# A fused scan-and-experts kernel: another order in the opening, weight sums two at a time, one set of scores two products sooner

## The chip, the cores and the metric

The kernel runs on one core of one Trainium2 chip. The metric is the time of one execution on the device in microseconds, the median of several runs. Five engines run side by side, each its own list of instructions in order: TensorE (PE, matrix products into PSUM banks; PEld is its loading of weights), VectorE (DVE), ScalarE (ACT), GpSimd (POOL) and SyncE (SP, which issues most transfers). ACT can issue transfers too. An engine waits on semaphores that other engines or transfers raise.

## The reference, cut to what matters

```python
# block 1: chunked scan; batch 4, 8 heads, 768 steps, head_dim 32, state 16
cum = np.cumsum(log(clip(a, 1e-6, 1)), -1)             # inside a chunk
L = np.exp(cum[..., :, None] - cum[..., None, :]) * causal
y = (C @ B.T * L) @ x + (C @ state) * exp(cum)         # per chunk
state = exp(cum[-1]) * state + (B * exp(cum[-1] - cum)).T @ x
# block 2: four experts on the 3072 x 256 tokens that y makes
p = probs / (probs.sum(-1, keepdims=True) + 1e-9)
for e in range(4):
    out += p[:, e:e+1] * (np.maximum(y @ w1[e], 0) @ w2[e])   # w1 256x1024, w2 1024x256
```

## The kernel before

**Work and tiles.** The 3072 steps are cut into 24 chunks of 128. Chunk `c` belongs to sequence `c % 4`. Everything is float32. The experts are computed with a fast matrix scheme of 20 products (`G`, blocks of three token pairs by four quarters of an expert's hidden units) and, for the very first expert of the first block, with smaller ones (`B`, 7 products, and plain products). Such a scheme multiplies sums of weight blocks with sums of token blocks. The weight sums are made once on the chip (`operands`, L1024, on POOL or DVE), used, stored to DRAM (`w_d`, L1029) and loaded again for the later token blocks. There are four token blocks of six chunks; each passes over all four experts.

**Two ways to the decay matrix.** For the first six chunks DVE multiplies up the decays themselves (`scan`, L519): of `a` with its first element of a row set to zero, spread over 128 partitions. For chunks 0 to 2 PE does the spreading (`spread`, L660) from three small tiles `aq0` and `aq1[:, 0:2]` (inside V buffers), in which only every 32nd partition holds a row and the others must be zero; for chunks 3 to 5 a transfer does it from a copy in DRAM, `acut_d` (`load_decays`, L463). Later chunks use logs: `a_sb` gets Ln on ACT (L708), DVE sums them (`sums`, L725), the sums go to `cum_d` in DRAM, and PE turns them for a bias (`bias`, L1360).

**The opening** (L568 to L738) is written out by hand, in program order for every engine. POOL and DVE clear `aq0` and `aq1`. SP loads the rows of `a` into `aq0` (L572), ACT loads `probs` (`pr`, L570) and the rows for `aq1` (L574). SP then loads `xb` (tokens, B and C of a chunk, in two parts for chunks 0 and 1), `a_sb` and the first weights. DVE clips the tiles between 1e-6 and `own`, which is one on every 32nd partition and zero elsewhere (L608). POOL adds up `probs` (`pairs`, `total_p`), DVE takes the reciprocal (L618), POOL makes the gates `pc` (L619), then clips `a_sb` and makes the cut copy `a_cut`, which SP stores to `acut_d` (L630). Then, for chunks 0 and 1: `spread` on PE, `mask` on ACT (L495), `score` on PE (L502), four scans per chunk on DVE (`scan_quarters`), and the product of scores and decays into `MT`. That product is made for each quarter `r` of the heads, either by `masked` (L681: DVE reads the scores in PSUM) or by `aside` (L675, L676: ACT copies the scores to a tile `gs`, POOL multiplies). Before, `aside` does quarters 0 and 1 of chunk 0 and quarter 0 of chunk 1; `masked` does the other five. `fade` (L540, POOL) adds the columns for the state, `inner` (L546, PE) makes the chunk's outputs and states, and ACT copies them out. `idle` (L684) are products of ones whose results nobody reads.

**The planned part.** What follows (from L743) is a list of works with costs per engine. A planner in the kernel's own Python (`Plan`) fixes the order on every engine before anything runs, from assumed costs, from the time `now` at which the planned part begins and from assumed times at which buffers and loads are ready. PE's order, `line`, is given; DVE, ACT, POOL and SP follow from latest starting times. `PAIRS_AT` says at which product of a unit (one expert over one token block) the scan's scores (`"s0"`) and outputs (`"o0"`) of the next block are put in. Since every engine's order comes out of one plan, a changed cost or start can move any instruction.

**Products.** `product` (L933) is the pair of 128x256 matmuls that nearly all of PE's time goes to. Between them DVE adjusts a bank (`adjust`, L1071), gates one (`gated`, L968) or combines sums (`combine`, L960), and ACT copies banks out and back (L942, L947, L1213).

Every transfer takes one of eight semaphores in turn, and its issue waits until the transfer that had that semaphore before has landed.

Of the kernel before, what the change touches and what calls it, by code (L numbers as in the profile page):

```python
# [8 lines left out]
FP32 = mybir.dt.float32  # L9
# [3 lines left out]
P = 128  # L13
# [18 lines left out]
URGENT = {}  # L32
# [3 lines left out]
SCANNED = 6  # L36
SCORED, OWN, LEAD, LEFT = 7, 4, 5, 3
FILLED = 3
HORIZON, OPENING, LOADED = 26.0, 80.0, 1.0
ORDERS = (0, 1, 2, 3), (3, 1, 2, 0), (0, 1, 2, 3), (3, 1, 2, 0)  # L40
PAIRS_AT = ((1, 24, "s0"), (2, 1, "o0"), (2, 1, "s1"), (2, 24, "s2"), (3, 1, "o12")), (
# [28 lines left out]
class Plan:  # L70
# [109 lines left out]
    def run(self, line, at, begin):  # L180
# [17 lines left out]
        self.stall, self.port, self.bus = [], 0.0, begin["SP"] + 4  # L198
# [103 lines left out]
class Scheme:  # L302
# [9 lines left out]
G.sums = ((15, 13, 10, -1), (9, 11, 10, -1), (0, "a", 16, -1), (2, "c", 11, -1), (1, "c", 13, -1),  # L312
          (14, 16, 13, -1), (3, "e", 10, -1), (7, 10, "c", -1), (18, "d", 10, -1), (17, "d", 16, -1),
          (8, 16, 11, -1), (19, "a", 13, -1), (6, "a", 11, -1), (12, 13, "d", -1), (5, "e", 16, -1),
          (4, 11, "e", -1))
# [6 lines left out]
G.shared = {1: ((15, 9), (0, 2), (1, 14), (3, 7), (18, 17), (8, 19), (5, 6), (12, 4)),  # L322
            2: ((9, 15), (7, 2), (19, 3), (17, 12), (14, 4), (8, 5), (18, 1), (6, 0))}
# [36 lines left out]
def kernel(  # L360
# [32 lines left out]
    def real(c):  # L393
        return c % NSEQ * NC + c // NSEQ
# [26 lines left out]
    def some(n, shape, name, pool=const):  # L421
# [19 lines left out]
        "dram": [None],  # L441
# [109 lines left out]
    def keep_state(c, A, y):  # L551
# [16 lines left out]
    nc.gpsimd.memset(aq0, 0.0)  # L568
    nc.vector.memset(aq1, 0.0)
    nc.scalar.dma_start(out=pr, in_=probs)  # L570
    a_rows = a.rearrange("(i k) (q t) s -> k q i (t s)", k=NC, t=NT)[0]
    nc.sync.dma_start(  # L572
        out=aq0.rearrange("(q r) t s -> q r (t s)", q=NQ)[:, 0], in_=a_rows[:, 0])
    nc.scalar.dma_start(  # L574
        out=aq1.rearrange("(q r) c t s -> q r c (t s)", q=NQ)[:, 0], in_=a_rows[:, 1:SPREAD])
# [3 lines left out]
    nc.sync.dma_start(out=xb[0][:, OBT:], in_=xbc[real(0)][:, OBT:])  # L579
    nc.sync.dma_start(  # L580
        out=a_sb, in_=a.rearrange("c h s -> (c h) s").rearrange("(p r) s -> p r s", r=2))
    nc.sync.dma_start(out=xb[1][:, OBT:], in_=xbc[real(1)][:, OBT:])
# [4 lines left out]
    load_tokens(2, xb[2])  # L587

# [4 lines left out]

    tmask = const.tile([P, NT], FP32)
    nc.vector.memset(tmask, 0.0)
    for q in range(NQ):
# [5 lines left out]
    own = const.tile([P, 1], FP32)  # L602
    nc.vector.reduce_sum(
        own.unsqueeze(2), ident[:, 0].rearrange("p (q r) -> p r q", r=32)[:, 0:1],
        axis=mybir.AxisListType.X)

    def clip(engine, v, top=1.0):
# [10 lines left out]
    nc.vector.reciprocal(total_p, total_p)  # L618
    nc.gpsimd.tensor_mul(  # L619
        pc.rearrange("p (k q) e -> p q k e", q=NSEQ), pr.rearrange("p (q k) e -> p q k e", q=NSEQ),  # L620
        total_p.rearrange("p (q k) e -> p q k e", q=NSEQ).to_broadcast([P, NSEQ, NC, E]))
    clip(nc.vector, aq1.rearrange("p c t s -> p (c t s)"), own)
    nc.vector.memset(aq1[:, :, :, 0:1], 0.0)

    clip(nc.gpsimd, a_sb)
    nc.gpsimd.tensor_copy(a_cut, a_sb)
    nc.gpsimd.memset(a_cut[:, :, 0:1], 0.0)

# [3 lines left out]

    store_decays(nc.sync, acut_d, a_cut)
    load_tokens(3, xb[3])
    for fb in range(2, 4):
        load_w1(fb, homes["W"][fb])
    for fb in range(4):
        load_w2(fb, homes["W"][4 + fb])
    load_decays(3, homes["ab"][0])
# [31 lines left out]
    gs = [homes["W"][-1][:, NT * P * i:NT * P * (i + 1)].rearrange("p (t s) -> p t s", t=NT) for i in range(2)]  # L671
# [21 lines left out]
    idle(BANK[7], 3)  # L693
    spread(0, four)
    idle(BANK[6], 3)
    mask(0, ctm[0], xb[0])
    score([0], ctm[:1], xb[:1], seven)
    scan_quarters(0, LT[0], four, 0)
    aside(0, 0, seven[0])
    aside(0, 1, seven[1])  # L700
    scan_quarters(0, LT[0], four, 1)
    fade(0, MT[0], xb[0], LT[0])
    mask(1, ctm[1], xb[1])
    spread(1, four)
    for r in (2, 3):
        masked(0, r, MT[0], LT[0], seven[r], 0)
    turn_gates(BANK[7])
    nc.scalar.activation(out=a_sb, in_=a_sb, func=AF.Ln)  # L708
    next_ = [BANK[4], BANK[0], BANK[1], BANK[6]]
    scan_quarters(1, LT[1], four, 0)  # L710
    score([1], ctm[1:], xb[1:2], next_)
    aside(1, 0, next_[0])
    y = BANK[7][:, :NT * (P + N)].rearrange("p (t s) -> p t s", t=NT)
# [6 lines left out]
    spread_gate(BANK[5], homes["gate"][0])  # L720
    for r in (3, 1, 2):
        masked(1, r, MT[1], LT[1], next_[r], 0)
    sums = homes["cum"][1]
    for r in range(2):
        nc.vector.tensor_tensor_scan(  # L725
            out=sums[:, r], data0=a_sb[:, r], data1=zeros[:NCH * NH // 2], initial=0.0,
            op0=ALU.add, op1=ALU.add)
    store_decays(nc.sync, cum_d, sums)
    ys = []
    for t in range(NT):  # L730
        y = BANK[6 + t][:, :P + N]
        ys.append(y)
        inner(1, t, y, xb[1], MT[1], P + N, True)
        nc.scalar.copy(out=yT0[:, t, P:], in_=y[:, 0:P])
# [3 lines left out]
    nc.sync.dma_start(out=p_d.rearrange("e c s -> c e s"), in_=p_sb)  # L738
# [6 lines left out]
    now = 13.2  # L745
# [25 lines left out]
    aq = plan.taken("V", NV - 2, 0.0)  # L771
    plan.homes["V"][NV - 4].free = now + 3.0
    plan.homes["W"][NW - 1].free = now
# [3 lines left out]
    st[3]["ab"] = plan.taken("ab", 0, now + 5.9)  # L777
# [4 lines left out]
    cum, cd, neg = plan.taken("cum", 1, now), plan.taken("dram", 0, now + 3.0), value("neg")  # L782

    def fetch(c):
# [9 lines left out]
        if "ab" not in s and c >= SPREAD:  # L794
            s["ab"] = value("ab")
            dma(lambda e: load_decays(c, s["ab"].t), 1, 512, part=[s["ab"]],
                reads=[cd] if c >= SCANNED else [])
# [184 lines left out]
    def source(fb, l, i):  # L982

        e, f = divmod(fb, EPB)
        if l == 1:
            return w1[e, i * P:i * P + P, f * FB:f * FB + FB]
# [577 lines left out]
```

## Time and profile before

| what | value |
|---|---|
| median of 3 runs | 612.39 us (612.10 to 612.56) |
| the profiled execution | 612.72 us, its span 610.9 us |
| PE | 603.7 us busy, 99% |
| DVE, ACT, POOL | 489.8, 292.9, 158.8 us |
| transfers | 99.65 MB, mean 163 GB/s |
| granted clock of PE | 1.0 |

Line numbers are those of the kernel before. A timeline line gives start, duration, engine, line, operation, tiles and count, and in brackets the idle time ahead of it with what ended it; several instructions may be merged into one line, which then runs from the first start to the last end. A line of the waits gives the engine and line that waited, for whom, the total, the number of times and the longest. A line of the windows gives the busy time of each engine, the granted clock, the share of the 16 DMA engines and GB/s. Matmuls are pipelined, so a busy PE may still run below its pace.

### The profile page before, as it was taken

The numbers are of one execution on the slowest core, as the hardware profiler recorded it, in microseconds if no ns is written. First come the engines' busy times: TensorE is split into PE (matmuls) and PEld (weight loads), VectorE is DVE, ScalarE is ACT, GpSimd is POOL, SyncE is SP. The second block draws the span as 40 slices with busy tenths as digits, with TensorE's granted clock in tenths as the row PEclk, the third lists the DMA queues.
The fourth block names the chain that finished last, engine by engine and source line by source line (L and its number), as shares of the span: only waits on it lengthen the run. The fifth ranks groups of instructions, "written<-read, shape, count | busy, mean of one in ns | idle before, by whom it ended". The sixth has DMA issues, their size and how long they took to land.

```text
span 610.9 us, 10142 instructions
## 1 busy us (share of the span) xinstructions
PE 603.7 (99%) x3365; PEld 513.6 (84%) x3365; DVE 489.8 (80%) x854; ACT 292.9 (48%) x681; POOL 158.8 (26%) x238
## 2 busy tenths in 40 slices
PE   9999999999999999999999999999999999999997
PEld 5778778888888888888888888888888888888885
DVE  7899997988879894887969988396785989575775
ACT  5267365487642327868352334734444142434441
POOL 6565546556461001676400100200000000000000
PEclk9999999999999999999999999999999999999999
DMA  7757668566853429893332425863142232953001
GB/s 253 257 185 222 194 215 326 187 213 228 285 160 98 113 36 328 280 313 124 134 117 87 149 47 140 274 237 118 55 127 80 87 91 63 341 187 121 1 0 53
DMA packets 89060, 99.65 MB, mean 163 GB/s; under 512 B 27428, under 2 KB 58928, under 8 KB 89008
## 3 DMA queue, kind: packets, MB, share of 16 engines
q1 hardware_dynamic: 88852, 98.95, 51.3%
q8 instruction: 27, 0.44, 0.3%
q14 instruction: 25, 0.20, 0.1%
q10 hardware_dynamic: 156, 0.06, 0.0%
HBM read 78.80 MB, written 20.17 MB: 162 GB/s over the span
## 4 chain that ended last, share of the span: by engine, by line
PE 92%; DVE 2%; ACT 1%; issue 0%; DVEq 0%
PE bank L933 88%; PE bank L546 2%; PE bank L502 1%; PE bank L879 1%; ACT A L556 1%; DVE v L968 1%; DVE v L960 0%; DVE MT L856 0%; ACT v L894 0%; DVE bank L1071 0%; DVE v L1260 0%; PE bank L1325 0%; DVE v L1425 0%; ACT LT L894 0%; ACT v L1330 0%
## 5 line engine op out<-in xcount | busy, mean ns | idle before, releaser
L933 PE MATMUL bank<-v,w 128*128 128x256 f32 x1676 | 394.8, 380 | 0.8 <-DVE bank L1071 0.7
L933 PEld LDWEIGHTS bank<-v,w 128*128 128x128 f32 x1676 | 316.9, 190 | 48.2 <-issue 2.2
L933 PE MATMUL bank<-Y,w 128*128 128x256 f32 x692 | 177.6, 381 | 0.7 <-ACT LT L894 0.4
L1213 ACT COPY v<-bank 128x512 f32<-128x512 f32 x109 | 64.0, 587 | 178.5 <-PE bank L933 166.2
L933 PEld LDWEIGHTS bank<-Y,w 128*128 128x128 f32 x692 | 130.2, 190 | 22.4 <-issue 2.0
L968 DVE SCALAR_TENSOR_TENSOR v<-bank,gate 128x512 f32<-128x512 f32 x149 | 102.3, 688 | 42.6 <-PE bank L933 39.7
L960 DVE TENSOR_TENSOR v<-v,v 128x512 f32<-128x512 f32 x181 | 126.6, 719 | 1.7 <-ACT v L942 0.3
L1071 DVE TENSOR_TENSOR bank<-bank,v 128x512 f32<-128x512 f32 x84 | 57.4, 696 | 35.7 <-PE bank L933 23.4
L942 ACT COPY v<-bank 128x512 f32<-128x512 f32 x100 | 58.6, 587 | 54.0 <-PE bank L933 45.0
L1024 POOL TENSOR_TENSOR w<-w,w 128x256 f32<-128x256 f32 x94 | 73.1, 794 | 42.5 <-DVE v L960 14.5
L947 ACT COPY bank<-v 128x512 f32<-128x512 f32 x127 | 74.0, 595 | 10.7 <-DVE v L968 8.7
L933 PE MATMUL bank<-LT,w 128*128 128x256 f32 x208 | 52.7, 379 | 0.0
L526 ACT ACTIVATE MT<-ab,neg 128x128 f32<-128x128 f32 x144 | 47.1, 396 | 2.1 <-DMA ab<-cum_d 2.1
L933 PEld LDWEIGHTS bank<-LT,w 128*128 128x128 f32 x208 | 39.4, 190 | 5.3
L531 POOL TENSOR_SCALAR_AFFINE_SELECT MT<-MT 128x512 f32<-128x512 f32 x36 | 23.2, 655 | 69.2 <-ACT MT L526 53.9
L1024 POOL TENSOR_TENSOR w<-w 128x256 f32<-128x256 f32 x32 | 24.3, 763 | 18.8 <-DVE Y L1043 7.7
L960 DVE TENSOR_TENSOR v<-bank,v 128x512 f32<-128x512 f32 x26 | 17.9, 688 | 11.1 <-PE bank L933 9.9
L856 DVE TENSOR_TENSOR MT<-bank,MT 128x512 f32<-128x512 f32 x36 | 22.7, 681 | 0.1
L1260 DVE TENSOR_TENSOR v<-v,v 128x256 f32<-128x256 f32 x55 | 21.1, 422 | 1.0 <-ACT v L1213 0.7
L960 POOL TENSOR_TENSOR v<-v,v 128x512 f32<-128x512 f32 x6 | 7.7, 1277 | 49.7 <-DVE v L960 49.7
L968 DVE SCALAR_TENSOR_TENSOR v<-v,gate 128x512 f32<-128x512 f32 x26 | 19.8, 763 | 0.4
L495 ACT ACTIVATE ctm<-xb,tmask 128x128 f32<-128x128 f32 x48 | 15.8, 395 | 3.8 <-DMA xb<-in_xbc_dram 3.7
(110 smaller groups left out, 315.1 us busy)
## 6 DMA issues: line engine op xcount, KB each, us to landing
w<-w_d SPq DMA_DIRECT2D x128, 256.0 KB
w_d<-w SPq DMA_DIRECT2D x64, 256.0 KB
w<-in_w_dram SPq DMA_DIRECT2D x40, 256.0 KB
ab<-cum_d SPq DMA_DIRECT2D x18, 512.0 KB
w<-in_w_dram SPq DMA_DIRECT2D x64, 128.0 KB
gate<-p_d SPq DMA_DIRECT2D x15, 384.0 KB
xb<-in_xbc_dram SPq DMA_DIRECT2D x17, 192.0 KB
out_dram<-v SPq DMA_DIRECT2D x144, 16.0 KB
```

The lines of the kernel that those rows point to most:

```text
L526: nc.scalar.activation(out=MT[:, place(c, h), 0:P], in_=ab[:, h * P:h * P + P], func=AF.Exp, bias=neg[:, h % NT, NQ * real(c) + h // NT:NQ ...
L531: nc.gpsimd.affine_select(out=MT[:, h:h + n, 0:P], in_=MT[:, h:h + n, 0:P], compare_op=ALU.is_ge, fill=0.0, base=0, pattern=[[0, n], [1, P ...
L856: nc.vector.tensor_mul(to, g, LT0[:, js, h] if cs[0] < SCANNED else to)
L933: nc.tensor.matmul(out=o, lhsT=w[:, j], rhs=x if half is None else x[:, j], start=(start and j == 0), stop=(j == 1), skip_group_check=True)
L942: act(.5, lambda e: nc.scalar.copy(out=flat(v), in_=bank.t), reads=[bank], writes=[v])
L947: act(.54 if to - lo > FB else .32, lambda e: nc.scalar.copy(out=bank.t[:, lo:to], in_=flat(v)[:, lo:to]), reads=[v], writes=[bank])
L960: plan.add(engines, lambda e: (on(e).tensor_add if sign > 0 else on(e).tensor_sub)(flat(v), whole(x), whole(y)), reads=[x, y], writes=[v], ...
L968: dve(D512, lambda e: nc.vector.scalar_tensor_tensor(out=h.t, in0=whole(x).rearrange("p (j m) -> p j m", j=JJ), scalar=0.0, in1=g.t[:, 2 * ...
L1024: plan.add(B256, lambda e, r=r, x=x, y=y, sign=sign: (on(e).tensor_add if sign > 0 else on(e).tensor_sub)(view(r), view(x), view(y)), two= ...
L1071: dve(D512, lambda e: (nc.vector.tensor_add if sign > 0 else nc.vector.tensor_sub)(to.t, bank.t, whole(x)), reads=[x, bank], writes=[to])
L1213: act(.5, lambda e: nc.scalar.copy(out=flat(v), in_=bank.t), reads=[bank], writes=[v], hold=HOLD)
L1260: plan.add(engines, lambda e: (on(e).tensor_add if sign > 0 else on(e).tensor_sub)(o[1](), x[1](), y[1]()), reads=[v for v in vs if v is n ...
```

## The change

Three groups of edits, and new constants for the planner.

1. *The opening.* The tiles `aq0` and `aq1` are no longer cleared; instead each load of rows of `a` fills all 128 partitions, every row repeated over 32 of them, and clipping with `own` makes the others zero. The two loads for `aq1` go ahead of `probs` on ACT's queue. On DVE, `own` is made first, and the second clip comes ahead of the reciprocal. On POOL the gates come behind `a_cut`, whose store moves from SP's to ACT's queue. All four quarters of chunk 0 are done by `aside`, the masks of chunk 1 come ahead of the first scores, and the spread of chunk 2 comes ahead of chunk 1's outputs. Ln and the sums of logs, their store and that of the gates move into the planned part. SP's order changes: the load from `acut_d` for chunk 3 goes ahead of the first `w2` loads.
2. *Weight sums two at a time.* Seven of the nine entries of `G.sums` now make two sums in one instruction of 512 columns. For this the raw blocks are loaded as pairs (`load_pair`), in place of whole or half tiles; the pairs stored together change.
3. *Scores.* `PAIRS_AT` puts the scores of the second block's first pair at product 22 of its unit in place of 24.

```diff
-HORIZON, OPENING, LOADED = 26.0, 80.0, 1.0
+HORIZON, OPENING, LOADED = 26.0, 80.0, -1.0
-PAIRS_AT = ((1, 24, "s0"), ...
+PAIRS_AT = ((1, 22, "s0"), ...
...
+G.ends = ("a", "c"), ("d", "e")
-G.sums = ((15, 13, 10, -1), (9, 11, 10, -1), (0, "a", 16, -1), ...
+G.sums = (((15, 9), (13, 11), 10), (0, "a", 16), ((1, 2), "c", (13, 11)), ...
...
-    nc.gpsimd.memset(aq0, 0.0)
-    nc.vector.memset(aq1, 0.0)
-    nc.scalar.dma_start(out=pr, in_=probs)
     nc.sync.dma_start(
-        out=aq0.rearrange("(q r) t s -> q r (t s)", q=NQ)[:, 0], in_=a_rows[:, 0])
-    nc.scalar.dma_start(
-        out=aq1.rearrange("(q r) c t s -> q r c (t s)", q=NQ)[:, 0], in_=a_rows[:, 1:SPREAD])
+        out=aq0.rearrange("p t s -> p (t s)"),
+        in_=a_rows[:, 0].unsqueeze(1).to_broadcast([NQ, 32, NT * P]))
+    for c in range(1, SPREAD):
+        nc.scalar.dma_start(
+            out=a_q[c].rearrange("p t s -> p (t s)"),
+            in_=a_rows[:, c].unsqueeze(1).to_broadcast([NQ, 32, NT * P]))
+    nc.scalar.dma_start(out=pr, in_=probs)
...
+    clip(nc.vector, aq1.rearrange("p c t s -> p (c t s)"), own)
+    nc.vector.memset(aq1[:, :, :, 0:1], 0.0)
     nc.vector.reciprocal(total_p, total_p)
...
     idle(BANK[6])
-    idle(BANK[7], 3)
+    idle(BANK[7], 2)
     spread(0, four)
-    idle(BANK[6], 3)
     mask(0, ctm[0], xb[0])
+    mask(1, ctm[1], xb[1])
     score([0], ctm[:1], xb[:1], seven)
     scan_quarters(0, LT[0], four, 0)
     aside(0, 0, seven[0])
     aside(0, 1, seven[1])
+    store_decays(nc.scalar, acut_d, a_cut)
     scan_quarters(0, LT[0], four, 1)
-    fade(0, MT[0], xb[0], LT[0])
-    mask(1, ctm[1], xb[1])
     spread(1, four)
     for r in (2, 3):
-        masked(0, r, MT[0], LT[0], seven[r], 0)
-    turn_gates(BANK[7])
-    nc.scalar.activation(out=a_sb, in_=a_sb, func=AF.Ln)
+        aside(0, r, seven[r])
+    fade(0, MT[0], xb[0], LT[0])
+    turn_gates(seven[0])
+    load_decays(3, homes["ab"][0])
+    for fb in range(4):
+        load_w2(fb, homes["W"][4 + fb])
...
-    now = 13.2
+    now = 11.9
...
+    def load_pair(v, fbs, l, f, i):
+        e, fb = divmod(fbs[f], EPB)
+        if l == 1:
+            nc.sync.dma_start(out=v.t, in_=w1[e, i * P:i * P + P, fb * FB:fb * FB + 2 * FB])
+        else:
+            nc.sync.dma_start(
+                out=v.t.rearrange("p (j m) -> p j m", m=P),
+                in_=w2[e, fb * FB:fb * FB + 2 * FB, i * P:i * P + P].rearrange("(j p) m -> p j m", p=P))
...
+                if isinstance(r, tuple):
+                    plan.add(B512, lambda e, r=r, x=x, y=y: difference(e, both(r), both(x), both(y)),
+                             two=True, reads=[where[x], where[y]], part=[where[r]], lean=True)
...
+    act(.3, lambda e: nc.scalar.activation(out=a_sb, in_=a_sb, func=AF.Ln), writes=[logs])
+    for r in range(2):
+        dve(.35, lambda e, r=r: sum_logs(e, r), reads=[logs], part=[cum])
+    dma(lambda e: store_decays(nc.sync, cum_d, cum.t), kb=96, reads=[cum], writes=[cd])
```

## The prediction

> **What bounds the kernel now.** I read the page first, then the waits of PE, the timeline of the first 13 us, the windows of DMA and last the timeline around the longest wait. From the page:
>
> ```profile
> span 610.9 us, 10142 instructions
> PE 603.7 (99%) x3365; PEld 513.6 (84%) x3365; DVE 489.8 (80%) x854; ACT 292.9 (48%) x681; POOL 158.8 (26%) x238
> PE 92%; DVE 2%; ACT 1%; issue 0%; DVEq 0%
> ```
>
> PE is the bound, and the chain that ended last is PE for 92% of the span. A PE that is always busy leaves two places where time can move: before its long run begins, and its waits inside it. The waits of PE, whole execution:
>
> ```profile
> PE bank L684 <- PEq L1556: 0.8, 1, 0.8
> PE bank L1325 <- DVE v L1260: 0.7, 1, 0.7
> PE bank L933 <- DVE bank L1071: 0.7, 1, 0.7
> PE bank L933 <- ACT LT L894: 0.4, 1, 0.4
> PE bank L502 <- ACT p_sb L647: 0.4, 1, 0.4
> ```
>
> Between the opening and the last 10 us, 1.1 us of waits are named (L1071, L894). So the body can give about 1 us. The opening is the rest. Its timeline:
>
> ```profile
> 0.81 0.40 ACTq L570 DMA_DIRECT2D pr<-in_probs_dram  x1
> 1.14 0.72 SPq L572 DMA_DIRECT2D v<-in_a_dram  x1
> 1.50 1.19 ACTq L574 DMA_DIRECT2D v<-in_a_dram  x1
> 2.67 0.27 POOL L614 TENSOR_TENSOR pairs<-pr 128x48 f32<-128x48 f32 x1 [0.22 <-DMA pr<-in_probs_dram]
> 3.25 0.35 DVE L608 TENSOR_SCALAR v<-v,own 128x256 f32<-128x256 f32 x1 [1.01 <-DMA v<-in_a_dram]
> 3.77 0.30 DVE L618 RECIPROCAL total_p<-total_p 128x24 f32<-128x24 f32 x1
> 4.67 1.07 POOL L608 TENSOR_SCALAR cum<-cum 96x256 f32<-96x256 f32 x1
> 4.68 2.43 DVE L519 TENSOR_TENSOR_SCAN LT<-bank,ident 128x256 f32<-128x256 f32 x4 [0.17 <-PE bank L660]
> 10.21 1.09 DVE L681 TENSOR_TENSOR MT<-bank,LT 128x256 f32<-128x256 f32 x3
> 12.61 3.72 PE L933 MATMUL bank<-v,w 128*128 128x256 f32 x16
> ```
>
> The long run of PE begins at 12.61. DVE's chain leads there: load of `a` (waited for until 3.25), scans from 4.68, last masked product done at 11.3, then PE and two copies of ACT, 1.3 us.
>
> **The change part by part.**
>
> **Loads of `a`.** Before, three sets of four 1 KB rows are loaded into tiles that a memset has cleared. After, each of the three loads writes 128 partitions, read from four rows of DRAM repeated 32 times: 131 KB each, 393 KB in all, one on SP's queue and two on ACT's, and `probs` is issued behind them. The kernel of before has loads of that form: `ah` (L469), four rows of DRAM repeated 16 times. The first two go at 19.46 and 20.1; the windows of DMA in which the second one's packets move, and of a second full of 128-row loads:
>
> ```profile
> 21.44:21.88 0.44, 0.44 (x3) 0.39 (x3) 0.44 (x2) 0.26 (x1) 0.17 (x1) 1.00 0.29 93
> 5.00:6.00 1.00, 1.00 (x11) 0.52 (x10) 1.00 (x3) 0.00 (x0) 0.94 (x2) 1.00 1.00 348
> ```
>
> The last two columns are the share of the 16 DMA engines and GB/s. The repeated load keeps 0.29 of the engines busy, four and a little, at 93 GB/s; ordinary loads fill all 16 at 348. So each of the three loads needs 131 KB / 93 GB/s = 1.4 us on four engines, not 0.4 us. Whether all three sit on the same four no row shows. Bounds: own fours each, 1.4 us for one; the same four, 4.2 us for three. I take the same four, since loads of one shape have nothing to tell them apart. [...]
>
> Now the sum. Both queues issue at about 0.8 (SP no longer waits for the memset). `ah` was issued at 19.46 and its first packet stands at 20.86, 1.4 us on; so data moves from 2.2. Up to `probs` the four engines must carry 393 KB, their quarter of what SP issues meanwhile (`xb` 131 + 131 + 197 KB and `a_sb` 98 KB: 139 KB) and of `probs` (12 KB): 544 KB / 93 GB/s = 5.85 us, until 8.05. `ah` landed 0.35 us behind its last packet, so `probs` lands at 8.4, where it was read at 2.67. If ACT's queue went first, `probs` would land at 2.2 + 405 / 93 + 0.35 = 6.9; I take equal turns.
>
> Who waits: on POOL, `pairs` starts at 8.5, its three operations take 1.07 (2.67 to 3.74), so the clip of `a_sb` starts at 9.6 (before 4.67). On DVE the reciprocal now stands ahead of the first scan, behind the clip of the second tile: 9.9, scans from 9.95 (before 4.68). Before, the same reciprocal was hidden in the wait for PE.
>
> **Masked products off DVE.** Two products of chunk 0 leave DVE (7.03 to 7.68: 0.65 us of its chain) for two more copies on ACT (0.33 each) and two more products on POOL (0.69 each). DVE needs 2.35 + 2.42 + 1.09 = 5.9 from first scan to last product: done at 15.85. POOL, from its clip: 1.69 to the end of `a_cut` (4.67 to 6.36), `pc` 0.5, four products 2.75, fade 0.4: 9.6 + 5.35 = 14.95. PE then runs, in order, chunk 0's outputs (0.63, as 9.10 to 9.73), the spread of chunk 2 (0.65, now ahead of chunk 1's outputs) and chunk 1's outputs, and 1.05 with ACT's copies to the long run: 17.3. DVE's own path gives 17.0. So the long run starts at 17.3 against 12.61: **+4.7 us**. With the lower bound for `probs` it is +3.2. With own fours the last load moves from 2.9 to 4.3 and `probs` lands near 4.9, with `xb` beside it: POOL's clip at 6.05, long run at 13.8, +1.2.
>
> **Memsets, idle matmul.** 0.31 on POOL, 0.48 on DVE and one warm-up product on PE go; all lie in waits for loads: 0. PE is then idle for some microseconds of the opening, and its first products ran slowly (two, of 512 and 384 columns, take 3.2 us at 0.84; one of 384 takes 0.9 at 4.59), so the small ones may run slower for a while: 0 to +0.5, taken 0, as they lie under DVE and POOL.
>
> **Sums of logs.** Ln (0.42 on ACT) and two scans (0.73 on DVE) move behind the start of the long run. PE's transposes of them come 3.55 us into it (12.61 to 16.16). ACT ends its masks of chunk 2 1.2 into it, Ln at 1.6, scans at 2.4: 1.1 us of cover, cost 0; behind those scans on DVE stand the first gated products, needed 5 us later. The store and the loads of `cum` are later on SP by as much; `ah` was read at 22.3 and its result first used by PE near 34.
>
> **Store and load of the cut decays.** The store goes to ACT's queue, where two copies stand behind it; the load that reads it passes four weight loads on SP. Before, DVE waited 2.1 us for it (17.2 to 19.2) and PE lost 0.2 later. Bounds 0 and -0.3; taken -0.2.
>
> **Sums two at a time.** 126 sums of 256 columns on POOL (97 us) become 50 of 512 (1.28 each by the row of L960 on POOL) and 30 of 256: 87 us; on DVE 18 become 8, 8 us become 5. POOL is 26% busy and PE names no wait for it: 0. Twice as long an operation can hold back another on DVE: +0.3 at most. The pair loads move the same bytes in 33 fewer issues; weights hold up no matmul in PE's waits: 0.
>
> **Scores two products sooner.** The longest wait inside the run:
>
> ```profile
> 69.21 1.15 PE L502 MATMUL bank<-ctm,xb 32*128 32x256 f32 x16
> 70.28 1.99 PE L933 MATMUL bank<-v,w 128*128 128x256 f32 x8
> 70.93 0.68 DVE L856 TENSOR_TENSOR MT<-bank,MT 128x512 f32<-128x512 f32 x1
> 72.13 0.69 DVE L1071 TENSOR_TENSOR bank<-bank,v 128x512 f32<-128x512 f32 x1
> 72.97 1.32 PE L933 MATMUL bank<-v,w 128*128 128x256 f32 x5 [0.69 <-DVE bank L1071]
> ```
>
> PE waits for an adjustment that stands in DVE's queue behind six others. In the order of the changed kernel the scores come ahead of the product that it adjusts, and only three operations, 1.8 us, stand between it and the adjustment before it (six, 3.6 us, before): PE has three products, 2.6 us, to cover them. I take -0.9 (0.69 and the slower restart of 0.2); bounds -1.0 and 0. The rest of the order is planned anew: as much as 0.5 either way.
>
> **Sum.** +4.7 - 0.2 - 0.9 = +3.6. The profiled execution took 612.72 (610.9 and 1.8 around it), 0.33 above the median: 616.3 on its own scale, **616.0** on the median's.
>
> **The rivals.**
>
> **Own fours, or little sharing.** For it: each load has its own queue place, and nothing shows the engines' numbers. Against: three loads on two queues must then spread over 12 engines by themselves. +1.2 - 1.1 = +0.1: 612.5, from 611.6 to 613.4.
>
> **Faster: the loads run on all 16 engines.** The place is the 393 KB at the head of the queues. At 348 GB/s they need 1.1 us, `probs` lands near 3.5 (issued at 1.7, 1.8 to landing as in the row of L570), POOL's clip starts at 4.7, the long run at 12.4: -0.2, with the body -1.3: 611.1, down to 610.5 if PE's other waits go too. It decides as long as `probs` lands before 4.8: later than that, POOL's chain (long run 8.9 us after the landing) eats the body's 1.1 us. For it: the destination has 128 partitions, where `ah` has 64. Against: the third `ah` load has eight rows and 128 partitions, and still about half the engines (window 22.05 to 22.59: 0.49).
>
> **Slower still: the sums of logs stand in PE's way.** If Ln comes more than 1.1 us later than worked out, as behind a late `xb` of chunk 2, PE's transposes wait, and all behind them: +1 to +2, 617 to 618.5.
>
> **How the numbers follow.** 0.66 for the forecast (614 to 617.4; the lower end is ACT's queue first, 614.4, and a body that gives 0.4 more), 0.14 for own fours, 0.14 for faster, 0.06 for slower still. About 0.2%, 1.2 us, is what a measurement of this kernel can tell from no change. Own fours lie mostly within it (0.10 of 0.14, 0.01 below, 0.03 above). So faster 0.15, same 0.10, slower 0.66 + 0.06 + 0.03 = 0.75. The range from 611.5 to 617.4 leaves out the faster case and most of the last.
>
> **What would show it.** Right: the clip of the first `a` tile (DVE, after the load) near 5.4 and not 3.25; the clip of the second near 8.3; `pairs` on POOL waiting for `probs` until 8.5; DVE idle before its first scan at about 9.9; the first long product at 17; a DMA share well under half between 2.2 and 5; no wait of PE for the adjustment near 76. Wrong: `pairs` before 5, or a first long product before 13.5; then the width of the loads is the failed step. If the opening is late as said and the total is not, the body gave more than 1.1 us and my bound on it failed.

## The result and the profile after

The changed kernel takes 621.12 us (median of 6 runs, 620.65 to 624.13), the kernel before 612.38 (6 runs on the same chip): ratio 1.0151, interval 1.0131 to 1.0170. It is slower by 8.7 us, where +3.6 was forecast, and it lies above the range. The profiled execution took 621.0 us, its span is 619.3, 8.32 longer than that of before (610.94).

From the page (PEclk is the granted clock of PE in forty slices, in tenths):

```profile
span 619.3 us, 9984 instructions
PE 605.4 (98%) x3363; PEld 515.7 (83%) x3363; DVE 491.5 (79%) x837; ACT 292.6 (47%) x683; POOL 157.6 (25%) x197
PEclk7899999999999999999999999999999999999999
PE 95%; DMA 1%; ACT 1%; DVE 1%; issue 0%; ACTq 0%; POOL 0%
```

The PEclk row has changed: before, all forty digits were 9. The timeline of the opening, line for line with the one of before:

```profile
6.05 0.35 DVE L612 TENSOR_SCALAR v<-v,own 128x256 f32<-128x256 f32 x1 [3.75 <-DMA v<-in_a_dram]
9.37 0.49 DVE L612 TENSOR_SCALAR v<-v,own 128x512 f32<-128x512 f32 x1 [2.83 <-DMA v<-in_a_dram]
9.82 0.27 POOL L618 TENSOR_TENSOR pairs<-pr 128x48 f32<-128x48 f32 x1 [7.62 <-DMA pr<-in_probs_dram]
10.79 0.30 DVE L624 RECIPROCAL total_p<-total_p 128x24 f32<-128x24 f32 x1 [0.80 <-POOL total_p L621]
10.83 1.07 POOL L612 TENSOR_SCALAR cum<-cum 96x256 f32<-96x256 f32 x1
11.01 4.70 DVE L519 TENSOR_TENSOR_SCAN LT<-bank,ident 128x256 f32<-128x256 f32 x8
16.54 2.08 PE L648 MATMUL bank<-p_sb,ident 96*128 96x128 f32 x8
16.71 1.09 DVE L678 TENSOR_TENSOR MT<-bank,LT 128x256 f32<-128x256 f32 x3 [1.00 <-PE bank L502]
19.67 1.24 PE L656 MATMUL bank<-v,const-float32-1.0 32*128 32x256 f32 x8
22.66 0.70 PE L934 MATMUL bank<-v,w 128*128 128x256 f32 x2 [1.11 <-ACT A L556]
```

Each step of the forecast's first chain is there and each is late: the clips at 6.05 and 9.37 (forecast 5.4 and 8.3), `pairs` at 9.82 (8.5), the first scan at 11.01 (9.95). The share of the DMA engines from 2.2 to 5 us, which was to be well under half, is 0.49. But the largest gap lies behind the scans: the long run starts at 22.66, not at 17.3. The windows of that stretch say why (columns as before; clock, DMA share and GB/s are the last three):

```profile
2.20:5.50 3.30, 1.54 (x3) 0.34 (x1) 0.10 (x1) 1.28 (x1) 0.00 (x1) 1.00 0.54 123
9.40:14.00 4.60, 2.31 (x7) 1.98 (x8) 3.73 (x9) 1.07 (x4) 3.81 (x9) 0.50 0.77 250
14.00:20.90 6.90, 6.55 (x48) 3.63 (x49) 2.79 (x6) 1.68 (x5) 5.35 (x10) 0.50 0.64 205
20.90:24.00 3.10, 1.99 (x23) 1.56 (x23) 2.76 (x5) 2.54 (x11) 0.50 (x2) 0.99 1.06 386
```

In the first window PE is busy for 1.54 of 3.30 us. Then, from 7.3 to 20.9, the granted clock is 0.50. The eight products that spread the gates (L648) take 2.08 us; the same eight took 1.16 before (L652, from 9.73 on). The waits of PE, without two that before had too (0.8 at the very start, 0.4 ahead of scores): the first two are in the opening (3.4 until 11.69, for the first scan; 2.9 until 6.59, for the first load of `a`), the third is at the start of the long run, the others are inside it:

```profile
PE bank L656 <- DVE LT L519: 3.4, 1, 3.4
PE bank L656 <- DVE v L615: 2.9, 1, 2.9
PE bank L934 <- ACT A L556: 1.1, 1, 1.1
PE bank L1346 <- DVE LT L1281: 0.7, 1, 0.7
PE bank L934 <- ACT v L895: 0.4, 1, 0.4
PE bank L934 <- DVE v L969: 0.2, 1, 0.2
```

The 0.7 for an adjustment (L1071 before, L1092 now) is gone. Behind the scores that were moved, PE goes on at once:

```profile
76.81 1.15 PE L502 MATMUL bank<-ctm,xb 32*128 32x256 f32 x16
77.89 1.13 PE L934 MATMUL bank<-Y,w 128*128 128x256 f32 x4
78.86 5.34 PE L934 MATMUL bank<-v,w 128*128 128x256 f32 x24
```

From the first long product to the end the span needs 596.60 us, before 598.33: -1.73.

### The profile page after: what moved, and what is told of

Same layout as the page of the kernel before. It is cut to its first block, busy times and chain, and to the rows that moved or that the text cites. A ratio compares the mean times of both kernels' runs of the same rounds, so it can differ in the third digit from the quotient of the medians.

```text
span 619.3 us, 9984 instructions
## 1 busy us (share of the span) xinstructions
PE 605.4 (98%) x3363; PEld 515.7 (83%) x3363; DVE 491.5 (79%) x837; ACT 292.6 (47%) x683; POOL 157.6 (25%) x197
## 4 chain that ended last, share of the span: by engine, by line
PE 95%; DMA 1%; ACT 1%; DVE 1%; issue 0%; ACTq 0%; POOL 0%
PE bank L934 90%; PE bank L546 2%; PE bank L502 2%; DMA pr<-in_probs_dram 1%; PE bank L880 1%; ACT A L556 1%; PE bank L656 1%; ACT v L895 0%; PE bank L648 0%; DVE v L969 0%; ACTq L573 0%; PE bank L1346 0%; DVE v L1281 0%; DVE LT L519 0%; DVE Y L1064 0%
## 5 line engine op out<-in xcount | busy, mean ns | idle before, releaser
L1234 ACT COPY v<-bank 128x512 f32<-128x512 f32 x106 | 62.1, 586 | 173.5 <-PE bank L934 167.3
L969 DVE SCALAR_TENSOR_TENSOR v<-bank,gate 128x512 f32<-128x512 f32 x147 | 100.9, 687 | 43.2 <-PE bank L934 40.1
L961 DVE TENSOR_TENSOR v<-v,v 128x512 f32<-128x512 f32 x172 | 122.0, 726 | 1.2 <-ACT v L943 0.2
L994 POOL TENSOR_TENSOR w<-w,w 128x512 f32<-128x512 f32 (+1 forms) x76 | 84.7, 1126 | 52.6 <-DVE v L961 16.6
L1092 DVE TENSOR_TENSOR bank<-bank,v 128x512 f32<-128x512 f32 x83 | 56.8, 696 | 37.0 <-PE bank L934 23.3
L943 ACT COPY v<-bank 128x512 f32<-128x512 f32 x101 | 59.1, 587 | 48.5 <-PE bank L934 40.1
L934 PE MATMUL bank<-LT,w 128*128 128x256 f32 x212 | 54.2, 379 | 0.0
L1234 ACT COPY LT<-bank 128x512 f32<-128x512 f32 x15 | 8.8, 587 | 26.4 <-PE bank L934 20.6
L961 DVE TENSOR_TENSOR v<-v,LT 128x512 f32<-128x512 f32 x23 | 18.6, 811 | 0.1
```

Of the source, the lines that this page charges most:

```text
L934: nc.tensor.matmul(out=o, lhsT=w[:, j], rhs=x if half is None else x[:, j], start=(start and j == 0), stop=(j == 1), skip_group_check=True)
L943: act(.5, lambda e: nc.scalar.copy(out=flat(v), in_=bank.t), reads=[bank], writes=[v])
L961: plan.add(engines, lambda e: (on(e).tensor_add if sign > 0 else on(e).tensor_sub)(flat(v), whole(x), whole(y)), reads=[x, y], writes=[v], ...
L969: dve(D512, lambda e: nc.vector.scalar_tensor_tensor(out=h.t, in0=whole(x).rearrange("p (j m) -> p j m", j=JJ), scalar=0.0, in1=g.t[:, 2 * ...
L994: (on(e).tensor_add if sign > 0 else on(e).tensor_sub)(out, x, y)
L1092: dve(D512, lambda e: (nc.vector.tensor_add if sign > 0 else nc.vector.tensor_sub)(to.t, bank.t, whole(x)), reads=[x, bank], writes=[to])
```

## The experiments

Theory after the result: the loads are later than forecast by some 1 us, and PE, idle while it waits for them, then runs at half clock until 21, which costs some 4 us more (clock theory). First rival: the new order of the opening, with its hand-overs between PE, ACT and POOL, costs those 4 us whatever the clock (order theory). Second rival: the loads are late for their bytes, place or issue, not for their width.

**rows.** Is it the width of the loads?

```diff
+    for q in range(NQ):
         nc.sync.dma_start(
-            out=aq0.rearrange("p t s -> p (t s)"),
-            in_=a_rows[:, 0].unsqueeze(1).to_broadcast([NQ, 32, NT * P]))
+            out=aq0[32 * q:32 * q + 32].rearrange("p t s -> p (t s)"),
+            in_=a_rows[q, 0].unsqueeze(0).to_broadcast([32, NT * P]))
...
+    for q in range(NQ):
         nc.scalar.dma_start(
+            out=aq1[32 * q:32 * q + 32].rearrange("p c t s -> p c (t s)"),
+            in_=a_rows[q, 1:SPREAD].unsqueeze(0).to_broadcast([32, SPREAD - 1, NT * P]))
```

> The changed kernel with one edit: each load of rows of a is cut into one transfer per row (four for the first tile, four for the two others together), so that the outermost size on both sides is 32 and not 4; bytes and row repeats are the same. Width theory (a load with four source rows runs on four engines, all loads of that shape on the same four): the first clip starts near 4.5 (6.05 in the changed kernel), the second near 5.5 (9.37), the first scan near 6.2 (11.01); the long run then starts near 13.6 if the granted clock stays up, near 18 if it is halved, total 612 or 616.5. Rival (the loads are late for their 393 KB, for their place in the queues or for their issue, not for their width): the second clip stays near 9, total 620 to 622.

618.41 us, ratio 1.0095 (1.0080 to 1.0110). Its timeline:

```profile
0.80 2.98 ACTq L574 DMA_DIRECT2D v<-in_a_dram  x4
4.95 0.35 DVE L613 TENSOR_SCALAR v<-v,own 128x256 f32<-128x256 f32 x1 [2.64 <-DMA v<-in_a_dram]
6.75 0.49 DVE L613 TENSOR_SCALAR v<-v,own 128x512 f32<-128x512 f32 x1 [1.32 <-DMA v<-in_a_dram]
8.62 4.69 DVE L519 TENSOR_TENSOR_SCAN LT<-bank,ident 128x256 f32<-128x256 f32 x8
14.15 2.08 PE L649 MATMUL bank<-p_sb,ident 96*128 96x128 f32 x8
```

The second clip moves from 9.37 to 6.75 with the same bytes: width is a real part, 2.6 us. It is not all: 5.5 was expected, and in the kernel before it stood at 3.99. ACT needs 2.98 us to issue its four loads, and the windows from 3 to 13 us show the 16 engines at 0.82 to 0.96. So both theories hold in part; how much of the rest is the 393 KB in place of 12 KB and how much the issue, this run does not separate. And the gates' products take 2.08 again: half clock.

**old_loads.** The loads of before in the changed kernel.

```diff
+    nc.gpsimd.memset(aq0, 0.0)
+    nc.vector.memset(aq1, 0.0)
+    nc.scalar.dma_start(out=pr, in_=probs)
     nc.sync.dma_start(
-        out=aq0.rearrange("p t s -> p (t s)"),
-        in_=a_rows[:, 0].unsqueeze(1).to_broadcast([NQ, 32, NT * P]))
+        out=aq0.rearrange("(q r) t s -> q r (t s)", q=NQ)[:, 0], in_=a_rows[:, 0])
...
-    nc.scalar.dma_start(out=pr, in_=probs)
```

> The changed kernel with the loads of a, the load of probs and the clearing of the tiles as in the kernel before; all else of the change stays. If the loads and the idle TensorE behind them are the whole loss: first scan near 4.7, long run near 12.1, total 610.5. If the new order of the opening costs 4 us by itself, or the clock falls without the removed idle product: first scan near 4.7, long run near 16, total 614.5; the granted clock between 8 and 12 us tells these two apart (1.0 in the first, 0.5 in the second).

614.90 us, ratio 1.0046 (1.0031 to 1.0062). The first scan is at 4.50, and yet the long run starts at 15.93. Between 9 and 11 us the granted clock is 0.50. So the second reading holds: even with loads in time the clock falls.

**warm.** Late loads, but PE kept at work.

```diff
     idle(BANK[7], 2)
+    fill(BANK[6], 5)
     spread(0, four)
...
     score([0], ctm[:1], xb[:1], seven)
+    fill(BANK[6], 8)
```

`fill` makes products of ones of 256 columns in the unused half of a bank.

> The changed kernel with products of ones in TensorE's two long gaps: five of 256 columns ahead of the first spread, eight behind the first scores. No load or other order is changed. Clock theory (idle from 3.7 to 6.6 keeps the granted clock at half until 21, and that costs some 4 us between first scan and long run): clock 1.0 from 5 on, first scan still near 11.0, long run near 18.5 (22.66 in the changed kernel), total 617. Order theory (the hand-overs of the new order cost it, not the clock): clock 1.0, long run near 22, total 620.5.

618.81 us, ratio 1.0095 (1.0079 to 1.0111). In the profile the first scan is at 10.35 and the long run at 18.86:

```profile
14.70 1.16 PE L648 MATMUL bank<-p_sb,ident 96*128 96x128 f32 x8
15.79 0.70 PE L546 MATMUL bank<-MT,xb 128*32 128x144 f32 x16
17.06 0.70 PE L546 MATMUL bank<-MT,xb 128*32 128x144 f32 x16
18.83 0.40 ACT L495 ACTIVATE ctm<-xb,tmask 128x128 f32<-128x128 f32 x1
18.86 0.48 PE L943 MATMUL bank<-v,w 128*128 128x256 f32 x1 [1.09 <-ACT A L556]
```

The gates' products are back at 1.16. From the first scan to the long run it takes 8.51 us in place of 11.65: the halved clock costs 3.1 us, the clock theory's amount less one. But the profiled execution is the fastest of the four: it took 617.1 at a mean granted clock of 1.000, the other three 618.7 to 619.0 at 0.996, so part of the clock was lost in them, where, no trace shows. By the medians the fills give back 2.3 us (621.12 to 618.81), midway between the clock theory's 617 and the order theory's 620.5; the clock and the stretch in the trace are what decides between the two.

**before_repeat.** Only the repeated loads, in the kernel before.

```diff
-    nc.gpsimd.memset(aq0, 0.0)
-    nc.vector.memset(aq1, 0.0)
-    nc.scalar.dma_start(out=pr, in_=probs)
...
+        in_=a_rows[:, 0].unsqueeze(1).to_broadcast([NQ, 32, NT * P]))
...
+    nc.scalar.dma_start(out=pr, in_=probs)
```

> The kernel before with only the repeated loads of a, probs behind them and no clearing of the tiles; opening order, sums and scores as before. Loads and clock theory: first scan near 11, granted clock half until 18 or later, long run at 11 + 7.9 + 3 to 4, near 22.5, total 622. Order theory (half of the loss belongs to the new order of the opening): long run at 11 + 7.9 = 19, total 618.8.

620.25 us, ratio 1.0121 (1.0104 to 1.0138). First scan 11.40, long run 21.70, granted clock 0.50 from 9 to 21. The loads with the clock that they cost are nearly all of the loss. The order theory's long run at 19 is out; the total, 1.75 below the other theory's 622, is only 1.45 above its 618.8. This kernel has all the products of ones of before, and its clock is at half all the same.

**before_less_idle.** Only the cut in the products of ones, in the kernel before.

```diff
-    idle(BANK[7], 3)
+    idle(BANK[7], 2)
     spread(0, four)
-    idle(BANK[6], 3)
```

> The kernel before with TensorE's products of ones cut as the change cuts them: the second one has 256 columns and not 384, the third (384 columns, behind the first spread) is left out. Nothing else is changed. Idle theory (these products keep the granted clock up through the scans of the opening): eight products of the gates take 2.1 us in place of 1.16, the long run starts 2.4 later, near 15, total 614.8. Rival (they lie in waits and are worth nothing, as the forecast had it): long run 12.6, total 612.4.

614.86 us, ratio 1.0038 (1.0023 to 1.0053).

```profile
11.54 2.08 PE L652 MATMUL bank<-p_sb,ident 96*128 96x128 f32 x8
15.78 3.50 PE L932 MATMUL bank<-v,w 128*128 128x256 f32 x15
```

One product of ones shortened from 384 to 256 columns and one of 384 left out, results that nobody reads, and the kernel is 2.3 us slower: the gates' products take 2.08, the long run starts at 15.78. The windows name a clock of 1.00 all the same: the column stands at 1.00 until the first recorded change. The durations tell: eight products of the scores take 1.24 us at 5.08 and again at 9.26, in before 0.71 at 5.44 and at 8.46.

**old_loads_idle.** Loads and products of ones of before, the rest as changed; the diff is against old_loads.

```diff
-    idle(BANK[7], 2)
+    idle(BANK[7], 3)
     spread(0, four)
+    idle(BANK[6], 3)
```

> The changed kernel with the loads of the kernel before and also its products of ones (384 columns in the second, the third back behind the first spread). Idle theory (loads and the cut products of ones are the whole loss): clock up, first scan 4.6, long run near 13 (8.5 behind it, as with the filled gaps), total 611.5. Order theory (the new order spreads chunk 1 at the pace of the scans and leaves TensorE too little to do, whatever stands ahead): clock half from 7 on, long run near 16, total 614.9.

613.22 us, ratio 1.0008 (0.9999 to 1.0018). First scan 5.35, long run 13.92, gates' products 1.16. With loads and products of ones restored, 7.9 of the 8.7 us are gone. The total lies midway between the two theories, 1.7 above 611.5 and 1.7 below 614.9. What decides is the clock: the gates' products are at 1.16, and the long run is nearer to 13 than to 16, so the order theory is out. Of the 0.9 that the long run is later than 13, the first scan has 0.75 (5.35 in place of 4.6).

**old_loads_fill, fill_outputs.** More products of ones, one behind each spread of chunk 1; then (the lines with `spread(2, third)`, fill_outputs alone) also the spread of chunk 2 behind the outputs.

```diff
     for q, b in enumerate(banks):
...
+            fill(BANK[6], n)
...
-    spread(1, four)
+    spread(1, four, 1)
...
+    fill(BANK[6], 3)
     turn_gates(seven[0])
+    fill(BANK[6], 1)
...
-    spread(2, third)
     ys = []
...
+    spread(2, third)
     for t, y in enumerate(ys):
```

> As old_loads_idle, and a product of ones of 256 columns behind each of the four spreads of chunk 1, three ahead of the turning of the gates and one behind it. Idle theory and order theory alike: clock up, long run near 13, total 611.5; if the clock is up and the long run is still near 15, hand-overs of the new order cost 2 us by themselves.

> As old_loads_fill, with the spread of chunk 2 put behind the outputs of chunk 1 again, as in the kernel before. Where the long run waits 1.1 us for ScalarE's copies of chunk 1's state, the spread (0.65 us) fills that wait: long run 0.65 earlier than in old_loads_fill, near 12.3, total 610.8. Rival (the outputs wait for the last masked products anyway, so their place is worth nothing): no difference.

617.23 (ratio 1.0084, 1.0067 to 1.0101) and 617.72 (1.0080, 1.0062 to 1.0097), both misses. The fills themselves came into the way: a spread and a fill in turn take 1.25 us where a spread took 0.6, and ACT's copy from the fills' bank waited 3.1 us for them. They say nothing on the order; a filler belongs where PE waits for long, not between products that others wait for.

**before_22, before_sums, before_body.** The two edits of the planned part, alone and together, with the opening of before (`PAIRS_AT` 24 to 22; `G.sums`, `G.shared`, `load_pair` and `operands` as in the change).

> The kernel before with one edit: the scores of the second block's first pair at product 22 of their unit. Forecast's step: the wait of TensorE for the adjustment near 73 (0.7) goes, -0.9, total 611.5. Rival (the order planned anew around it puts another wait in its place): 612.3 to 612.7.

> The kernel before with only the weight sums two at a time (their loads as pairs with them). Forecast's step: 0, at most +0.3, total 612.4 to 612.8, and the wait near 73 stays. Rival (the part of the body's gain that the scores don't explain, some 0.8, comes from here): 611.6.

> The kernel before with the sums two at a time and the scores at product 22, its opening and its planner's constants untouched. If all that the change loses is lost in the opening, the body's -1.7 remains: total 610.8, faster than both kernels. Rival (the gain of the body came with the new opening: buffers free earlier, planner's constants): 612.4.

| kernel | us, ratio to before | long product to long product, summed |
|---|---|---|
| before | 612.54 | 556.72 |
| before_22 | 612.19, 0.9996 (0.9987 to 1.0004) | 555.90 |
| before_sums | 614.61, 1.0033 (1.0022 to 1.0044) | 558.35 |
| before_body | 613.75, 1.0021 (1.0012 to 1.0030) | 557.44 |

The third column adds up, in the profiled execution, the times from the start of one long product to that of the next where nothing else stands between them on PE. The scores give -0.82 there, as forecast (-0.9), and PE's wait of 0.7 for the adjustment is gone. In the total they can't be told from no change: 0.35 less, with an interval from 0.8 less to 0.2 more, and the profiled opening was 0.66 longer. The sums alone cost +1.63 there:

```profile
PE bank L933 <- DVE bank L1091: 2.2, 2, 1.2
50.38 1.44 DVE L960 TENSOR_TENSOR v<-v,v 128x512 f32<-128x512 f32 x1
51.73 0.69 DVE L1091 TENSOR_TENSOR bank<-bank,v 128x512 f32<-128x512 f32 x1
52.57 0.67 PE L933 MATMUL bank<-Y,w 128*128 128x256 f32 x2 [1.01 <-DVE bank L1091]
```

PE waits twice for an adjustment; ahead of the one at 51.73 DVE has an operation of 1.44 us, twice the mean of its group on the page of before (0.72). That POOL, now in operations of 1.3 us, holds it up was not tried. So the body's gain does not survive in the old plan: before_body lies 2.95 above the 610.8 that was expected of it, and 1.35 above its rival's 612.4.

**one_at_a_time.** The changed kernel with the sums of before.

> The changed kernel with the weight sums one at a time, as in the kernel before; opening, scores and planner's constants as changed. If the pairs of sums cost the changed kernel what they cost the kernel before (+2.1, in TensorE's waits for adjustments behind them on VectorE): 619.0. If that cost came only from the old plan's order, as the changed kernel's few named waits say: 621, or a little more.

620.86 us, ratio 1.0135 (1.0120 to 1.0149), by 0.26 below the changed kernel's median, which its own runs can't tell from none. Its span from the first long product on is 596.92 (changed: 596.60). In the plan of the changed kernel the sums cost nothing that these runs can tell, in that of before they cost 2.

**outputs_first, best_fill, best_one.** In search of a version that beats both: old_loads_idle with the spread of chunk 2 behind the outputs of chunk 1; the same with two fills behind the first scores in place of the products of ones ahead of them; and that with the sums one at a time. The move of the spread is in all three, the fills are in the last two.

```diff
-    spread(2, third)
     ys = []
...
+    spread(2, third)
     for t, y in enumerate(ys):
...
     score([0], ctm[:1], xb[:1], seven)
+    fill(BANK[6], 2)
```

> As old_loads_idle, with the spread of chunk 2 behind the outputs of chunk 1 again. Order theory, small: the long run waits 1.1 us for ScalarE's copies of chunk 1's state, and the spread (0.65) fills that wait: long run 0.65 earlier, total 612.5 against 613.2. Rival (their place is worth nothing): long run at 13.9, total 613.2.

> The changed kernel with the loads of the kernel before, the spread of chunk 2 behind the outputs of chunk 1, and two products of ones of 256 columns behind the first scores (none ahead of them, where they held the scores back by 0.85). Idle theory: these are enough to keep the clock up; first scores at 5.0, long run near 12.8, total 611.7. Rival: too little work, clock half from 7 on, long run near 15.5, total 614.5.

> As best_fill, with the weight sums one at a time. If pairs of sums cost in this plan too: below best_fill by 1 to 2 us, near 610. If not: the same as best_fill or slower.

612.79 (1.0002, 0.9993 to 1.0011), 613.25 (1.0007, 0.9998 to 1.0015) and 612.72 (1.0011, 1.0000 to 1.0022). None is faster than the kernel before. In outputs_first the long run's wait for ACT fell from 1.1 to 0.5, but the outputs now wait 0.4 for POOL's `fade`, and the long run starts at 13.80 (old_loads_idle 13.92). In best_fill the clock rose, the gates' products took 1.16 and the long run started at 13.41, but PE then waited 1.0 once for DVE. best_one, with the sums one at a time, is 0.5 faster than best_fill by the medians; their intervals overlap.

**The stretch from the first scan to the first long product**, in the profiled executions of all but old_loads_fill and fill_outputs, which the fills stretch:

| kernel | opening | first scan | long run | between | gates' products |
|---|---|---|---|---|---|
| before | old | 4.68 | 12.61 | 7.93 | 1.16 |
| before_22 | old | 5.35 | 13.27 | 7.92 | 1.16 |
| before_sums | old | 4.94 | 12.86 | 7.92 | 1.16 |
| before_body | old | 4.72 | 12.65 | 7.93 | 1.16 |
| before_less_idle | old | 5.24 | 15.78 | 10.54 | 2.08 |
| before_repeat | old | 11.40 | 21.70 | 10.30 | 2.08 |
| old_loads_idle | new | 5.35 | 13.92 | 8.57 | 1.16 |
| warm | new | 10.35 | 18.86 | 8.51 | 1.16 |
| outputs_first | new | 4.66 | 13.80 | 9.14 | 1.16 |
| best_fill | new | 4.96 | 13.41 | 8.45 | 1.16 |
| best_one | new | 5.16 | 13.87 | 8.71 | 1.16 |
| rows | new | 8.62 | 19.54 | 10.92 | 2.08 |
| one_at_a_time | new | 10.43 | 22.19 | 11.76 | 2.08 |
| old_loads | new | 4.50 | 15.93 | 11.43 | 2.08 |
| after | new | 11.01 | 22.66 | 11.65 | 2.08 |

Whatever the loads do, the clock sets most of the stretch: 2.4 to 2.6 us between half and full in the old order, 2.4 to 3.2 in the new one (rows to one_at_a_time, against old_loads_idle); and the new order is 0.5 to 1.2 longer at the same full clock (0.6 in warm and old_loads_idle, which have the changed order itself).

## Why the prediction was wrong in size

The span's +8.32, term by term, from single profiled executions:

| term | forecast | measured |
|---|---|---|
| loads of `a`, to the first scan | +5.27 | +6.33 |
| first scan to long run: halved clock | 0 | +3.14 (11.65 - 8.51) |
| first scan to long run: order of operations | -0.58 | +0.58 (8.51 - 7.93) |
| long run to end | -1.1 | -1.73 |

**Loads of `a`: right in mechanism, 1.06 short.** The first load on ACT's queue, alone from 2.30 to 2.90, keeps 0.25 of the 16 engines busy, at 77 GB/s: a width of four. That the three loads share the same four was the author's choice, with no row of before to show it; the updates of the transfers' semaphores in the trace of the changed kernel bear it out (us):

```
second load for aq1   2.97 (one)               8.69  8.79  9.15  9.27
probs                 6.27 ... 7.01 (twelve)   9.17  9.19  9.63  9.74
xb of chunk 1         5.92 ... 6.74 (twelve)   8.08  8.23  8.43  8.58
```

A load with four source rows shows five updates, the first one early; `xb`, `probs` and `a_sb` show 16. The four loads with 16 updates issued next, from 2.31 to 3.40 (`xb` of chunk 1, `probs`, `a_sb` and the next `xb`), have exactly four late ones each, the first of them 1.3 to 2.2 us behind the twelfth: read as a quarter of each that queues behind the repeated rows, on the engines that these use. With own fours the last repeated load would have been done near 4.3, by the forecast's sum; its last update is at 9.27.

Mis-sized was the rate of the four engines. The 93 GB/s come from a window in which two packets of 4 KB of another transfer moved beside the 64 packets of 512 B of the repeated load; the load alone moved 33 KB in 0.44 us, 74 GB/s. The changed kernel's first load on ACT's queue has the same rate, 131 KB from 2.28 to 4.08, 73 GB/s. With 74 the forecast's sum gives 2.2 + 544 / 74 + 0.35 = 9.9 for `probs`, which landed at 9.74 (forecast 8.4). SP's first weights, issued at 6.04, did not hold `probs` up: their own four late updates come at 10.53 to 10.73. Some 0.6 us differ from one execution to another: in one_at_a_time, which has the same opening, `pairs` stands at 9.24 and the first scan at 10.43.

**Memsets, idle matmul: the step that failed.** "0 to +0.5, taken 0, as they lie under DVE and POOL" was the price of small products that run slower for a while; +3.14 was measured. They do not lie under DVE and POOL: at half clock the scores of chunk 1 come so late that DVE waits 1.00 for them (16.71), and then gates, outputs and spread follow one another on PE to the long run. What the forecast looked at was the length of the products taken away; what the runs price is the clock that they keep up, and they show it from both sides: leaving them out in the kernel before costs 2.3 us, filling the gaps in the changed kernel gives 3.1 of the stretch back (2.3 of the total by the medians), and putting them back with the old loads takes the total from 614.90 to 613.22. In the changed kernel two causes meet, and each is enough alone: PE's idling for the late loads (before_repeat, all products of ones kept: 2.08) and the products taken away (before_less_idle, loads in time: 2.08). The timeline of before was enough to see the risk: first products "ran slowly" (two, of 896 columns together, 3.2 us at 0.84) and a later one did not (384 columns, 0.9 at 4.59). The traces show two states (the gates' products at 2.08 and at 1.16), and in the changed kernel the fall at 7.29, when PE had been busy for 0.70 of the last 3.41 us. What decides between the two they do not show, and how busy PE was does not tell it: in old_loads the clock falls at 7.28 though PE counts as busy for 2.89 of the 3.41 us before. In before_less_idle PE counts as busy for 3.00 of 3.00 us from 6 to 9, and for 5.00 of 5.00 to 14, and the gates' products at 11.54 still run at half: there, small products that follow one another at the pace of DVE did not lift the clock.

**Masked products off DVE: -0.58 forecast, +0.58 measured.** DVE and POOL did what the sum said (eight scans 4.70, three products 1.09). But two steps of PE were too short in it, as warm shows at full clock. Chunk 0's outputs start 5.44 behind the first scan (10.35 to 15.79; the sum has 5.00), since the scores of chunk 1 and the gates' products, from 14.06 to 15.86, stand ahead of them on PE; in the sum they waited for POOL alone. And from the start of chunk 1's outputs to the long run it takes 1.80 (17.06 to 18.86), not 1.05: in the new order ACT's copies stand bare, 1.1 us of PE's wait for `A`, since the spread of chunk 2, which covered them before, now comes ahead. Together that is +1.19, and 1.16 lie between forecast and measurement. outputs_first closed half of that wait and opened one for POOL: the order has little to give either way.

**Scores two products sooner: right in the body.** -0.9 forecast, -0.82 alone in the profiled body; the total does not confirm it. **Sums two at a time: right by the plan's luck.** 0 forecast, nothing that can be told here, +2.1 in the plan of before. **Sums of logs, store of the cut decays:** no wait of PE names them; no run tried them alone.

**Long run to end: -1.1 forecast, -1.73 measured.** Half of it need not be the edits'. before_less_idle and before_repeat, whose body is that of before, need 597.47 and 597.43 from the first long product to the end, where before needs 598.33: with a later start some 0.9 goes by itself, 0.58 of it in the first 48 long products. The forecast had no such term; which wait goes, no view names. The scores' -0.82 is about the rest.

**Rivals.** Own fours and all 16 engines fell with the second clip at 9.37. "Slower still" was right in sign and named the wrong mechanism, the sums of logs. The range ended at 617.4 because no case priced the clock.

## What to carry over

Before taking away a product of ones or letting PE wait in an opening, compare the durations of equal small products with and without work ahead of them (here 2.08 and 1.16 us for the gates' eight): the price was that of every PE step until the clock was back, 2.3 us in before_less_idle, not that of the piece removed. The first load on ACT's queue here, four source rows repeated over 128 partitions, moved its 131 KB with a quarter of the engines busy, at 73 GB/s, and the four transfers issued behind the repeated loads, on both queues, had four of their 16 updates late, by 1.3 us and more. A rate read from a window is that of all that moves in it: count the load's own packets. An edit to a planned order has no price of its own: the same sums cost 2 us in one plan and nothing in another, so its cost is read only from the order that it leads to.

## What the runs showed that was not expected

- The granted clock's column says 1.00 until a first change is recorded (in the changed kernel's trace a rise, at 3.87). In before_less_idle and rows it stands at 1.00 over stretches in which the gates' eight products took 2.08 us in place of 1.16, and one_at_a_time has a mean of 0.999 with the same 2.08. In the traces of before and of the changed kernel the changes lie whole multiples of 3.41 us apart (before: up at 3.74, down at 611.32; changed: up at 3.87, down at 7.29, up at 20.94). Where in the opening the clock rises differs from one execution of the same opening to another: chunk 0's spread took 0.71 us in the changed kernel (at 6.59) and 1.24 in one_at_a_time (at 6.47).
- One and a third products of ones of 384 columns in the first 6 us decide over 2.3 us. From the first scan on, one order repeats to 0.01 us at full clock (7.93, 7.92, 7.92 and 7.93 in before, before_22, before_sums and before_body), while the first scan itself moves with the spread on PE that it waits for: 4.68, 5.35, 4.94 and 4.72, after waits of 0.17, 0.87, 0.42 and 0.25. That spread took 0.71 us in before, at 3.95, and 1.24 in before_22, at 4.09.
- Issuing a repeated load takes ACT 0.87 us (two in 1.74), `probs` 0.49; so `probs` is issued at 2.58, not at 0.81, before its bytes wait for anything.
